# Attention probabilities stored token tile by token tile, and a PV matmul whose moving operand comes in four runs

## The chip, the cores and the metric

The kernel runs on one core of a Trainium2 chip. The metric is the device time of one execution in microseconds (us), as a median over executions. With one core, a run's state is judged by its distance from the fastest run of the same kernel.

The engines are named as in the profile: PE is TensorE (matmuls), PEld its weight loads, DVE is VectorE, ACT is ScalarE, POOL is GpSimd, and SP is the engine that issues most DMAs.

## The reference, cut to what matters

A layer-normed input of 2048 tokens goes through attention with 32 query heads over 8 cached key/value heads, of which the last W = 512 keys count, and through an MLP whose output gates the result.

```python
q = (xn @ wq).reshape(B, Sq, 32, 128).transpose(0, 2, 1, 3)   # B = 1, Sq = 2048
k = jnp.repeat(k_cache[:, :, Sk - 512:, :], 4, axis=1)
v = jnp.repeat(v_cache[:, :, Sk - 512:, :], 4, axis=1)
scores = jnp.einsum("bhqd,bhkd->bhqk", q, k) * (128 ** -0.5)
p = softmax(scores, axis=-1)                                  # the probabilities
o = jnp.einsum("bhqk,bhkd->bhqd", p, v)                       # "PV"
s = o.transpose(0, 2, 1, 3).reshape(B, Sq, 4096) @ wo
out = x + s * g                                               # g: the gate, from the MLP
```

## The kernel before

The tokens are cut into 4 blocks of 512, each block into 4 tiles of 128. One step of the main loop handles one head of one block (128 steps). For each token tile `j`, PE computes the scores of 128 tokens (on the partitions) against 512 keys; ACT takes the exponential and its row sum; DVE divides by the sum. The PV matmuls of this program read the keys on the partitions, so a DMA transpose, the "flip", turns the 16 blocks of 128 x 128 over. Four steps later PE multiplies the flipped probabilities by V, and DVE evicts the result.

```python
def score(s, j):
    h = s % HQ
    if j == 0:
        p_all[s] = work.tile([P, NKC, BLKT, P], BF16, name="p_all", tag="p_all", bufs=4)
        den[s] = work.tile([P, BLKT], FP32, name="den", bufs=3)
    sc = ps.tile([P, W], FP32, name="sc_ps", tag="sc", bufs=4)
    nc.tensor.matmul(sc, qT[s][:, j * P : (j + 1) * P], kT[h // REP], start=True, stop=True)
    nc.scalar.activation(
        p_all[s][:, :, j, :], sc.rearrange("p (kc q) -> p kc q", q=P),
        ACT.Exp, scale=INV_SQRT_DH, accum_out=den[s][:, j : j + 1],
    )

def normalise(s, j0, j1):
    rden = work.tile([P, 2], FP32, name="rden", bufs=4)
    nc.vector.reciprocal(rden, den[s][:, j0 : j1 + 1])
    for j in range(j0, j1 + 1):
        nc.vector.tensor_scalar_mul(
            p_all[s][:, :, j, :], p_all[s][:, :, j, :], rden[:, j - j0 : j - j0 + 1]
        )

def flip(s):
    pT[s] = work.tile([P, NKC, BLK], BF16, name="pT", tag="pT", bufs=4)
    nc.sync.dma_start_transpose(
        pT[s].rearrange("p kc (j q) -> p (kc j) q", q=P), p_all[s][:, :, :, :]
    )

# ... in pv_units, for kc in range(4) (chunks of 128 keys):
    nc.tensor.matmul(
        cur["ps"], v_sb[h // REP][:, kc, :], pT[s][:, kc, :], start=(kc == 0), stop=(kc == NKC - 1)
    )
    # ... after the last one:
    nc.vector.tensor_copy(oT[s // 2][:, s % 2, :], cur["ps"])
```

On each partition, `p_all` holds the 2048 probabilities of four token tiles in the order (key chunk, token tile, key). So the 512 probabilities of one tile lie in four runs of 128, while the flip leaves all 512 tokens of a key chunk in one run for PV.

The softmax here doesn't subtract the row's maximum and nothing guards it: scores larger than these inputs give would overflow.

Of the kernel before, what the change touches and what calls it, by code (L numbers as in the profile page):

```python
# [9 lines left out]
P = 128  # L10
# [3 lines left out]
BF16 = mybir.dt.bfloat16  # L14
# [8 lines left out]
def kernel(  # L23
# [17 lines left out]
    REP = HQ // HKV  # L41
    W = min(4096, max(256, SK // 4))
    NKC = W // P
# [3 lines left out]
    BLKT = 4  # L47
    BLK = BLKT * P
# [15 lines left out]
    work = ctx.enter_context(tc.tile_pool(name="work", bufs=2))  # L64
    ps = ctx.enter_context(tc.tile_pool(name="ps", bufs=1, space=bass.MemoryType.PSUM))
# [14 lines left out]
    v_sb = [res.tile([P, NKC, DH], BF16, name=f"v{g}", tag=f"v{g}") for g in range(HKV)]  # L80
# [119 lines left out]
    p_all = {}  # L200
    pT = {}
# [26 lines left out]
    def score(s, j):  # L228
        h = s % HQ
        if j == 0:  # L230
            p_all[s] = work.tile([P, NKC, BLKT, P], BF16, name="p_all", tag="p_all", bufs=4)
            den[s] = work.tile([P, BLKT], FP32, name="den", bufs=3)
        sc = ps.tile([P, W], FP32, name="sc_ps", tag="sc", bufs=4)
        nc.tensor.matmul(  # L234
            sc, qT[s][:, j * P : (j + 1) * P], kT[h // REP], start=True, stop=True
        )
        nc.scalar.activation(  # L237
            p_all[s][:, :, j, :],
            sc.rearrange("p (kc q) -> p kc q", q=P),
            ACT.Exp,  # L240
            scale=INV_SQRT_DH,
            accum_out=den[s][:, j : j + 1],
        )

    def normalise(s, j0, j1):
        rden = work.tile([P, 2], FP32, name="rden", bufs=4)
        nc.vector.reciprocal(rden, den[s][:, j0 : j1 + 1])  # L247
        for j in range(j0, j1 + 1):
            nc.vector.tensor_scalar_mul(  # L249
                p_all[s][:, :, j, :], p_all[s][:, :, j, :], rden[:, j - j0 : j - j0 + 1]  # L250
            )

    def flip(s):
        pT[s] = work.tile([P, NKC, BLK], BF16, name="pT", tag="pT", bufs=4)
        nc.sync.dma_start_transpose(
            pT[s].rearrange("p kc (j q) -> p (kc j) q", q=P), p_all[s][:, :, :, :]
        )

    s25 = {}
# [1 line left out]
    def row_sums(p):  # L261

        tag = ("kT", "v")[p % 2] + str(p // 2)
        s25[p] = res.tile([P, 2, HALF], BF16, name=f"s25_{p}", tag=tag)
        o = oT[(NBLK - 1) * HQ // 2 + p]
        nc.vector.tensor_tensor(
            out=s25[p].rearrange("p a b -> p (a b)"), in0=o[:, 0, :], in1=o[:, 1, :], op=ALU.add
        )

    def pv_units(s, tag="o"):  # L270
        b, h = divmod(s, HQ)
        cur = {}

        def mm(kc):
            if kc == 0:
                cur["ps"] = ps.tile([P, BLK], FP32, name="o_ps", tag=tag, bufs=1)
            nc.tensor.matmul(  # L277
                cur["ps"], v_sb[h // REP][:, kc, :], pT[s][:, kc, :], start=(kc == 0), stop=(kc == NKC - 1)
            )
            if kc == NKC - 1:  # L280
                if s % 2 == 0:
                    oT[s // 2] = work.tile([P, 2, BLK], BF16, name="oT", tag="oT", bufs=OT_BUFS // 2)
                nc.vector.tensor_copy(oT[s // 2][:, s % 2, :], cur["ps"])  # L283
                if b == NBLK - 1 and s % 2 == 1:
                    row_sums(h // 2)
                del pT[s], p_all[s], qT[s], den[s]

        return [lambda kc=kc: mm(kc) for kc in range(NKC)]
# [326 lines left out]
    with tc.manual_schedule(engines={ENG.PE, ENG.Activation, ENG.DVE, ENG.SP, ENG.Pool}):  # L615
# [161 lines left out]
        for s in range(NSTEP):  # L777
            b, h = divmod(s, HQ)
# [9 lines left out]
            def sc(j):  # L788
                score(s, j)
                if j == 0 and s >= 1:  # L790
                    normalise(s - 1, 2, 3)
                    flip(s - 1)
                if j == 2:
                    normalise(s, 0, 1)
                if j == 3 and s == NSTEP - 1:
                    normalise(s, 2, 3)
                    flip(s)
# [59 lines left out]
```

## Time and profile before

| | before |
|---|---|
| median | 550.09 us (549.88 to 551.0, 3 runs) |
| span of the profiled run | 547.7 us, granted PE clock (the share of its full clock that PE was let have) 1.000 |
| PE, DVE, ACT busy | 99%, 84%, 72% |
| PV matmuls | 512, 379 ns each on the record, 20% of the chain |
| normalising multiplies (DVE) | 512, mean 351 ns |
| exponentials (ACT) | 512, mean 597 ns |

First, lines of the profile page of the kernel before: busy time per engine; the chain of work that ended last; groups of instructions (line, engine, operation, output<-input, shapes, count | busy us, mean ns of one | idle of the engine just before them, and what ended it); and the flip with its median time to landing.

```profile
PE 542.2 (99%) x2676; PEld 261.1 (48%) x2676; DVE 458.4 (84%) x1258; ACT 392.1 (72%) x1125; POOL 20.5 (4%) x41
...
PE 98%; DMA 1%; SPq 0%; DVE 0%; issue 0%
...
L237 ACT ACTIVATE p_all<-sc_ps 128x512 bf16<-128x512 f32 x512 | 305.1, 597 | 104.4 <-PE sc_ps L234 100.4
L249 DVE TENSOR_SCALAR p_all<-p_all,rden 128x512 bf16<-128x512 bf16 x512 | 158.0, 351 | 9.1
L283 DVE CAST oT<-o_ps 128x512 bf16<-128x512 f32 x128 | 88.2, 689 | 35.8 <-PE o_ps L277 35.0
...
L277 PE MATMUL o_ps<-pT,v_100 128*128 128x512 bf16 x64 | 18.4, 379 | 0.0
...
pT<-p_all SPq DMA_TRANSPOSE x128, 4.4
```

A matmul's 379 ns on the record is not what it costs. The records overlap, so the cost is the distance from one start to the next. The records of DVE's multiplies overlap too: 512 of 351 ns would be 180 us, and the group is busy for 158. For PE the table of stages gives the distance (busy us and count per engine, granted clock, DMA share, GB/s):

```profile
core 0: us, PE busy (x) PEld busy (x) DVE busy (x) ACT busy (x) POOL busy (x), PEclk, DMA share, GB/s
...
100.00:240.00 140.00, 139.98 (x650) 63.37 (x649) 111.85 (x298) 101.49 (x290) 2.85 (x5) 1.00 0.86 170
240.00:380.00 140.00, 140.00 (x650) 63.48 (x649) 121.42 (x343) 108.32 (x325) 6.33 (x12) 1.00 0.87 164
```

140 us hold 650 matmuls, one per 215.4 ns, and PE is never idle. The timeline of PE in the kernel before shows the same for one group of PV matmuls (start us, us from the first start to the last end, what, count):

```profile
201.11 1.03 PE L277 MATMUL o_ps<-pT,v_99 128*128 128x512 bf16 x4
201.97 0.38 PE L234 MATMUL sc_ps<-kT_92,qT 128*128 128x512 bf16 x1
```

From 201.11 to 201.97 us is 0.86 us for four matmuls, 215 ns each. This way of reading, the start of the next group less the start of PV's group, divided by four, is used for every experiment below.

Finally, all that PE waited for in the kernel before (engine and line <- who: us, times, longest). Both entries belong to the first microseconds; in the main loop no matmul waits for DVE, ACT or a flip.

```profile
PE warm_ps L642 <- DVE eps L74: 1.2, 1, 1.2
PE h_ps L691 <- DMA w_0_111<-in_B_w_dram: 0.2, 1, 0.2
```

### The profile page before, as it was taken

To read this page: it belongs to the slowest core of one execution; us is meant where nothing else is said; L and a number is where in the kernel's file an instruction comes from. 1 tells how busy PE (TensorE), PEld (TensorE's weight loads), DVE (VectorE), ACT (ScalarE), POOL (GpSimd) and SP (SyncE) were. 2 spreads that over 40 slices of the span, in tenths; PEclk is the share of its full clock that TensorE was granted. 3 is DMA by queue.
4 is the path that set the end of the run, shared out by engine and by line. 5 is a ranking of instruction groups with operands and counts; after the bars stand their busy time and mean duration, and the time that the engine had idled before them with its cause. 6 is when DMAs were issued, how large, how long until landed. Compare 5 with 4: busy or idle time off the path is not lost.

```text
span 547.7 us, 8533 instructions
## 1 busy us (share of the span) xinstructions
PE 542.2 (99%) x2676; PEld 261.1 (48%) x2676; DVE 458.4 (84%) x1258; ACT 392.1 (72%) x1125; POOL 20.5 (4%) x41
## 2 busy tenths in 40 slices
PE   8999999999999999999999999999999999999997
PEld 5644444444444444444444444444444444444586
DVE  6888888887886788898889888988889889988897
ACT  5558757866875677777777777777788888888600
POOL 1000010000000000010001000100010000000010
PEclk9999999999999999999999999999999999999999
DMA  8969769778849799979887988798889778888921
GB/s 260 278 115 186 160 131 165 152 152 159 168 89 193 171 199 226 211 154 193 160 152 145 189 163 143 155 187 161 145 161 183 153 152 156 185 153 154 173 78 40
DMA packets 298909, 89.69 MB, mean 164 GB/s; under 512 B 282352, under 2 KB 297968, under 8 KB 298864
## 3 DMA queue, kind: packets, MB, share of 16 engines
q1 hardware_dynamic: 297056, 85.02, 79.2%
q0 software_dynamic: 1312, 3.67, 2.6%
q10 hardware_dynamic: 496, 0.46, 0.3%
q8 instruction: 21, 0.34, 0.2%
q14 instruction: 24, 0.20, 0.1%
HBM read 17.30 MB, written 2.10 MB: 35 GB/s over the span
## 4 chain that ended last, share of the span: by engine, by line
PE 98%; DMA 1%; SPq 0%; DVE 0%; issue 0%
PE o_ps L277 20%; PE q_ps L212 20%; PE sc_ps L234 20%; PE s_ps L335 15%; PE oB_ps L181 9%; PE h_ps L148 7%; PE m_ps L478 4%; PE h_ps L691 2%; DMA w_0_111<-in_B_w_dram 1%; SPq L622 0%; SPq L618 0%; SPq L623 0%; PE t_ps L658 0%; DVE m_4_6595 L502 0%; DVE x_t L604 0%
## 5 line engine op out<-in xcount | busy, mean ns | idle before, releaser
L237 ACT ACTIVATE p_all<-sc_ps 128x512 bf16<-128x512 f32 x512 | 305.1, 597 | 104.4 <-PE sc_ps L234 100.4
L249 DVE TENSOR_SCALAR p_all<-p_all,rden 128x512 bf16<-128x512 bf16 x512 | 158.0, 351 | 9.1
L283 DVE CAST oT<-o_ps 128x512 bf16<-128x512 f32 x128 | 88.2, 689 | 35.8 <-PE o_ps L277 35.0
L237 ACT ACTIVATION_READ_ACCUMULATOR p_all<-sc_ps 128x1 f32 x512 | 100.4, 196 | 0.0
L224 DVE CAST qT<-q_ps 128x512 bf16<-128x512 f32 x111 | 76.3, 687 | 3.3 <-PE q_ps L212 3.3
L234 PEld LDWEIGHTS <-qT 128*128 128x128 bf16 x512 | 50.1, 98 | 60.5 <-issue 0.2
L335 PEld LDWEIGHTS <-oT 128*128 128x128 bf16 x384 | 37.6, 98 | 45.3
L247 DVE RECIPROCAL rden<-den 128x2 f32<-128x2 f32 x256 | 40.5, 158 | 11.1 <-ACT p_all L237 10.9
L158 ACT ACTIVATE th<-h_ps 128x512 bf16<-128x512 f32 x42 | 25.0, 595 | 4.0 <-PE h_ps L148 3.9
L335 PE MATMUL s_ps<-wo_big_2344,oT 128*128 128x512 bf16 x84 | 26.0, 379 | 0.0
L335 PE MATMUL s_ps<-wo_big_2084,oT 128*128 128x512 bf16 x84 | 26.0, 379 | 0.0
L335 PE MATMUL s_ps<-wo_big_2345,oT 128*128 128x512 bf16 x84 | 26.0, 379 | 0.0
L335 PE MATMUL s_ps<-wo_big_2083,oT 128*128 128x512 bf16 x84 | 26.0, 379 | 0.0
L234 PE MATMUL sc_ps<-kT_91,qT 128*128 128x512 bf16 x64 | 24.3, 379 | 0.0
L234 PE MATMUL sc_ps<-kT_93,qT 128*128 128x512 bf16 x64 | 24.3, 379 | 0.0
L234 PE MATMUL sc_ps<-kT_95,qT 128*128 128x512 bf16 x64 | 24.3, 379 | 0.0
L234 PE MATMUL sc_ps<-kT_94,qT 128*128 128x512 bf16 x64 | 24.3, 379 | 0.0
L234 PE MATMUL sc_ps<-kT_96,qT 128*128 128x512 bf16 x64 | 24.3, 379 | 0.0
L234 PE MATMUL sc_ps<-kT_97,qT 128*128 128x512 bf16 x64 | 24.3, 379 | 0.0
L234 PE MATMUL sc_ps<-kT_92,qT 128*128 128x512 bf16 x64 | 24.3, 379 | 0.0
L234 PE MATMUL sc_ps<-kT_98,qT 128*128 128x512 bf16 x64 | 23.9, 379 | 0.0
L277 PE MATMUL o_ps<-pT,v_100 128*128 128x512 bf16 x64 | 18.4, 379 | 0.0
(316 smaller groups left out, 858.4 us busy)
## 6 DMA issues: line engine op xcount, KB each, us to landing
pT<-p_all SPq DMA_TRANSPOSE x128, 4.4
x_e<-in_A_x_dram POOLq DMA_DIRECT2D x12, 128.0 KB, 3.2
out_dram<-x_e POOLq DMA_DIRECT2D x12, 128.0 KB, 2.3
w_0_113<-in_B_w_dram SPq DMA_DIRECT2D x1, 896.0 KB, 8.9
w_1_114<-in_B_w_dram SPq DMA_DIRECT2D x1, 896.0 KB, 9.8
w_0_111<-in_B_w_dram SPq DMA_DIRECT2D x2, 256.0 KB, 5.1
w_1_112<-in_B_w_dram SPq DMA_DIRECT2D x1, 512.0 KB, 6.9
x_130<-in_A_x_dram SPq DMA_DIRECT2D x1, 512.0 KB, 8.8
```

The lines of the kernel that those rows point to most:

```text
L148: nc.tensor.matmul(h_ps[:, lo : lo + n], w1_sb[f // FH][:, c, (f % FH) * P : (f % FH + 1) * P], xnT[b][:, c, lo : lo + n], start=(c == 0), ...
L158: nc.scalar.activation(th, h_ps, ACT.Tanh, scale=0.5)
L181: nc.tensor.matmul(cur["ps"], hT[b][f // 2][:, f % 2, j * P : (j + 1) * P], w2_sb[f // FH][:, f % FH, :], start=(f == 0), stop=(f == NFC - 1),
L212: nc.tensor.matmul(cur["ps"], wq_sb[h // REP][:, c, (h % REP) * DH : (h % REP + 1) * DH], xnT[b][:, c, :], start=(c == 0), stop=(c == ND - 1),
L224: nc.vector.tensor_copy(qT[s], cur["ps"])
L234: nc.tensor.matmul(sc, qT[s][:, j * P : (j + 1) * P], kT[h // REP], start=True, stop=True)
L237: nc.scalar.activation(p_all[s][:, :, j, :], sc.rearrange("p (kc q) -> p kc q", q=P), ACT.Exp, scale=INV_SQRT_DH, accum_out=den[s][:, j : ...
L247: nc.vector.reciprocal(rden, den[s][:, j0 : j1 + 1])
L249: nc.vector.tensor_scalar_mul(p_all[s][:, :, j, :], p_all[s][:, :, j, :], rden[:, j - j0 : j - j0 + 1])
L277: nc.tensor.matmul(cur["ps"], v_sb[h // REP][:, kc, :], pT[s][:, kc, :], start=(kc == 0), stop=(kc == NKC - 1))
L283: nc.vector.tensor_copy(oT[s // 2][:, s % 2, :], cur["ps"])
L335: nc.tensor.matmul(acc[j], oT[(b * HQ + h) // 2][:, h % 2, j * P : (j + 1) * P], wo_of(h), start=(h == 0), stop=(h == HQ - 1),)
```

## The change

The intent is to let ACT and DVE write and read one run of 512 instead of four runs of 128. The price is that PV reads its moving operand in four runs of 128 (256 bytes), 1 KB apart. The flip covers the same contiguous 2048 columns on both sides; only the meaning of its 16 blocks changes.

```diff
-            p_all[s] = work.tile([P, NKC, BLKT, P], BF16, name="p_all", tag="p_all", bufs=4)
+            p_all[s] = work.tile([P, BLKT, W], BF16, name="p_all", tag="p_all", bufs=4)
@@ exp
-            p_all[s][:, :, j, :],
-            sc.rearrange("p (kc q) -> p kc q", q=P),
+            p_all[s][:, j, :],
+            sc,
@@ multiply
-                p_all[s][:, :, j, :], p_all[s][:, :, j, :], rden[:, j - j0 : j - j0 + 1]
+                p_all[s][:, j, :], p_all[s][:, j, :], rden[:, j - j0 : j - j0 + 1]
@@ flip
-        pT[s] = work.tile([P, NKC, BLK], BF16, name="pT", tag="pT", bufs=4)
+        pT[s] = work.tile([P, BLKT, NKC, P], BF16, name="pT", tag="pT", bufs=4)
-            pT[s].rearrange("p kc (j q) -> p (kc j) q", q=P), p_all[s][:, :, :, :]
+            pT[s].rearrange("p j kc q -> p (j kc) q"), p_all[s].rearrange("p j w -> p (j w)")
@@ PV
-                cur["ps"], v_sb[h // REP][:, kc, :], pT[s][:, kc, :], ...
+                cur["ps"], v_sb[h // REP][:, kc, :], pT[s][:, :, kc, :], ...
```

The two built programs, compared instruction by instruction, differ in 1536 places and in access patterns only: the output of 512 exponentials, both sides of 512 multiplies, and the moving operand of 512 PV matmuls. The score in PSUM is read as one run in both, and the flips are identical. Order and semaphores are the same.

More of the change, by code (lines that the diff above doesn't have):

```diff
@@ L277, in mm @@
             nc.tensor.matmul(
-                cur["ps"], v_sb[h // REP][:, kc, :], pT[s][:, kc, :], start=(kc == 0), stop=(kc == NKC - 1)
+                cur["ps"], v_sb[h // REP][:, kc, :], pT[s][:, :, kc, :], start=(kc == 0), stop=(kc == NKC - 1)
             )
```

## The prediction

> **What bounds the kernel now.** TensorE. The page's busy table gives PE 542.2 us of the 547.7 us span (99%), and the chain of waits is PE for 98%. In the table of stages PE is busy 139.98 of 140.00 us between 100 and 240 us, with 650 matmuls at a granted clock of 1.00: one per 215.4 ns.[...] PE's own waits sum to 1.4 us. DVE is busy 84%, ACT 72%, DMA queue 1 79%, but in the view of who waited for whom no matmul of the main loop waits for them.
>
> **What the change does.** The two built programs, compared by instruction, have the same 8,031 instructions in the same order with the same semaphores. Only access patterns differ, in three groups of 512.
>
> 1. Exp on ACT (mean 597 ns) writes one run of 512 instead of four of 128. Tanh of the same size, which already writes one run, takes 595 ns. Change: 0 to -2 ns each.
> 2. The normalising multiply on DVE (mean 351 ns, 158 us in all) reads and writes one run. Estimates from the trace: bf16 tensor_tensor takes 285, 422, 553 and 687 ns for 256, 512, 768 and 1024 elements: about 153 ns fixed[...]; runs of 256 lie on that line, so breaks are free there.[...] centering x, one run with two pointer scalars, takes 407. [...]I expect 340 to 352 ns. Were breaks what makes 351 out of 287, DVE would save at most 33 us, all off the critical path.
> 3. PV's moving operand becomes four runs of 128 bf16 (256 B), 1 KB apart. These 512 matmuls are 20.2% of the chain (512 x 215.4 ns = 110 us): the only term on the critical path. The trace has no matmul with such an operand.[...] I expect 0 to 2 ns per matmul, 0 to 1 us in all.
>
> The flip moves the same 16 blocks between the same addresses; its 4.4 us to landing should stay.
>
> **Predicted time:** 550.2 us, range 548.5 to 553.5 us. Faster by over 2%: 1%. Within 2%: 94%. Slower by over 2%: 5%.
>
> **What would show each step right or wrong.**
> - PV durations stay at 379 ns and their share of the chain at 20.2%; 650 matmuls fill 140 us. If PV grows, step 3 is wrong: 10 ns per PV matmul would be 5 us, 21 ns would pass 2%.
> - The multiply's mean at 340 to 352 ns; near 290 would mean that breaks did cost DVE, and its busy share would fall to about 78% with the span unchanged.
> - Exp at 595 to 597 ns; flip 4.4 us; no new PE wait.
>
> **What would make it wrong.** A fixed cost on PE for every break in the moving operand: at three breaks per matmul, 7 ns each is 2%. Or reads by PE at 1 KB steps[...], seen as spread in the PV durations (now 377 to 380 ns). Or a faster DVE that starts flips in another rhythm; nothing on PE waits for flips today, with four heads of lag, so that should not surface.

Passages of this text that no trace of this case showed are cut, with the cut marked, and terms of step 2's sum go with them. The sum came to about 347 ns: 153 fixed, 134 for 512 elements at half the 0.52 ns per element of the tensor_tensor rows, and about 60 for the pointer scalar; without the last it is the 287 that the text still names. The 0.52 is (687 - 285) / 768; the half of it was assumption, and so was the 60, the rest of 351 less 287. The total, 550.2 us, is within 0.2 us of the medians of the kernel before (550.09 and 550.04 us): steps 1 and 2 were put off the critical path, and step 3 added 0 to 1 us.

## The result

The changed kernel takes 549.90 us (median of 6 runs, 549.69 to 550.27); the kernel before, run beside it, 550.04 us (6 runs, 549.84 to 551.0). The ratio is 0.9997, with a 95% interval of 0.9984 to 1.0009: the same time. Ratios here and below are the mean time of one kernel's fast runs over the mean of the other's in the same rounds, so they are not quite the ratios of the quoted medians.

The page of the changed kernel, the same lines as above:

```profile
PE 542.3 (99%) x2676; PEld 261.5 (48%) x2676; DVE 458.1 (84%) x1258; ACT 391.9 (72%) x1125; POOL 20.5 (4%) x41
...
PE 99%; DVE 0%; ACT 0%; issue 0%
...
L237 ACT ACTIVATE p_all<-sc_ps 128x512 bf16<-128x512 f32 x512 | 305.1, 597 | 104.5 <-PE sc_ps L234 100.5
L249 DVE TENSOR_SCALAR p_all<-p_all,rden 128x512 bf16<-128x512 bf16 x512 | 157.9, 351 | 9.1
L283 DVE CAST oT<-o_ps 128x512 bf16<-128x512 f32 x128 | 88.2, 689 | 35.9 <-PE o_ps L277 35.2
...
L277 PE MATMUL o_ps<-pT,v_105 128*128 128x512 bf16 x64 | 18.4, 379 | 0.0
...
pT<-p_all SPq DMA_TRANSPOSE x128, 4.4
```

The table of stages, PE's timeline around one PV group, and PE's waits, all of the changed kernel:

```profile
100.00:240.00 140.00, 139.98 (x650) 63.33 (x648) 111.82 (x299) 101.23 (x290) 3.08 (x5) 1.00 0.88 170
240.00:380.00 140.00, 140.00 (x650) 63.47 (x649) 121.39 (x343) 108.52 (x325) 6.09 (x12) 1.00 0.87 165
```

```profile
200.87 1.03 PE L277 MATMUL o_ps<-pT,v_99 128*128 128x512 bf16 x4
201.74 0.38 PE L234 MATMUL sc_ps<-kT_92,qT 128*128 128x512 bf16 x1
```

```profile
PE warm_ps L642 <- DVE eps L74: 1.2, 1, 1.2
```

No instruction that the change touches became longer or shorter, to the nanosecond of its mean: 597, 351 and 379 ns before and after. Four PV matmuls still take 0.87 us to the next start; summed over all 512 PV matmuls of the trace, the distances to the next start are 110.6 us before and after. The 0.3 us between the two profiled spans (547.7 and 547.4 us) are within the spread of single runs.

The trace therefore shows no two opposed effects. The open questions are why a break between runs is free, how far that holds, and whether the time would have moved had DVE gained.

### The profile page after: what moved, and what is told of

Read it like the earlier page. It is cut to its first block, busy times and chain, and to the rows that moved or that the text cites. A ratio compares the mean times of both kernels' runs of the same rounds, so it can differ in the third digit from the quotient of the medians.

```text
span 547.4 us, 8533 instructions
## 1 busy us (share of the span) xinstructions
PE 542.3 (99%) x2676; PEld 261.5 (48%) x2676; DVE 458.1 (84%) x1258; ACT 391.9 (72%) x1125; POOL 20.5 (4%) x41
## 4 chain that ended last, share of the span: by engine, by line
PE 99%; DVE 0%; ACT 0%; issue 0%
PE sc_ps L234 20%; PE q_ps L212 20%; PE o_ps L277 20%; PE s_ps L335 15%; PE oB_ps L181 9%; PE h_ps L148 7%; PE m_ps L478 4%; PE h_ps L691 2%; PE warm_ps L642 1%; PE t_ps L649 0%; PE t_ps L658 0%; DVE m_4_6595 L502 0%; DVE x_t L604 0%; ACT xnT_107 L653 0%; DVE warm L68 0%
## 5 line engine op out<-in xcount | busy, mean ns | idle before, releaser
L249 DVE TENSOR_SCALAR p_all<-p_all,rden 128x512 bf16<-128x512 bf16 x512 | 157.9, 351 | 9.1
```

The source lines that it names most:

```text
L249: nc.vector.tensor_scalar_mul(p_all[s][:, j, :], p_all[s][:, j, :], rden[:, j - j0 : j - j0 + 1])
```

## The experiments

Theory: breaks between runs of 256 bytes cost nothing on any of the three engines; and PE's stream of matmuls alone sets the time, so DVE's and ACT's times do not matter. Rivals: a small loss on PE is paid back by a small gain elsewhere; or breaks do cost, too little to be seen at three per instruction; or DVE is part of what sets the time.

Twelve kernels ran, all against the kernel before. The three that compute wrong values (half_pv, half_prob, mul_imm) still came back as correct: the scores of this input are small, the softmax is nearly flat, and presumably the tolerance does not see whose key block was used (this was not tested). Correctness therefore proves nothing for those three. In the other nine it does not prove much more about which key is which, but their patterns are permutations of tokens or elementwise, and a wrong token order would be a wrong output row.

### The two halves of the change (half_pv, half_prob)

half_pv is the kernel before with only PV's new reading:

```diff
-   cur["ps"], v_sb[h // REP][:, kc, :], pT[s][:, kc, :], ...
+   cur["ps"], v_sb[h // REP][:, kc, :], pT[s].rearrange("p kc (j q) -> p kc j q", q=P)[:, :, kc, :], ...
```

> Only PV's part of the change: the kernel before, but each PV matmul reads four runs of 128 columns 1 KB apart, as in the changed kernel; it therefore reads blocks that belong to other keys, a wrong result on purpose. Theory (a break in the moving operand costs TensorE nothing, and every other part of the change costs nothing either): ratio to before 1.000 within 0.2%, PV matmuls 379 ns, PV 20.2% of the chain. Rival (PV got dearer and ACT or DVE paid it back, so that the sum is zero): this half alone is slower, by 0.5% or more, with PV matmuls above 379 ns or waits on PE.

Measured: 550.05 us against 550.18 us, ratio 0.9994 (0.9982 to 1.0007). PV is 20% of the chain, and its matmuls take 379 ns:

```profile
L277 PE MATMUL o_ps<-pT,v 128*128 128x512 bf16 x512 | 145.1, 379 | 0.3
```

half_prob is the changed kernel with PV reading one run of 512 again:

```diff
-   cur["ps"], v_sb[h // REP][:, kc, :], pT[s][:, :, kc, :], ...
+   cur["ps"], v_sb[h // REP][:, kc, :], pT[s].rearrange("p j kc q -> p (j kc q)")[:, kc * BLK : (kc + 1) * BLK], ...
```

> Only the probabilities' part of the change: exp and the multiply in one run of 512, flip as in the changed kernel, but PV reads one run of 512, hence the wrong blocks, a wrong result on purpose. Theory: ratio 1.000 within 0.2%, multiply 351 ns, exp 597 ns. Rival (the sum of the change is zero because this half gains): faster by 0.5% or more.

Measured: 549.95 us against 550.18 us, ratio 0.9991 (0.9977 to 1.0005); multiply 351 ns, exp 597 ns. Neither half moves the time, so the zero of the whole is not a sum of a loss and a gain. That rival falls. (The traces of half_pv, half_prob, pv_runs8 and pv_step8 lack 45 to 48 of the 2676 matmul records, while all 2676 weight loads are there, so matmuls per stage are not counted from these four.)

### How far a break is free on PE (pv_runs8, pv_step8, pv_runs2, pv_step2, pv_step4)

These are the kernel before with PV's 512 columns read in another order. The eviction writes them back to their places, so the result is right. The edit of pv_runs8; the others differ only in the pattern:

```diff
-   cur["ps"], v_sb[h // REP][:, kc, :], pT[s][:, kc, :], ...
+   cur["ps"], v_sb[h // REP][:, kc, :], pT[s][:, kc, :].rearrange("p (c r e) -> p r c e", r=8, e=8), ...
-   nc.vector.tensor_copy(oT[s // 2][:, s % 2, :], cur["ps"])
+   nc.vector.tensor_copy(
+       oT[s // 2][:, s % 2, :].rearrange("p (c r e) -> p r c e", r=8, e=8),
+       cur["ps"].rearrange("p (r c e) -> p r c e", r=8, e=8),
+   )
# pv_runs2: r=16, e=2.  pv_step8, pv_step4, pv_step2: "p (c r) -> p r c" with r=8, 4, 2
```

The first two:

(Cut from this group's expectations is a rule about reads within 16 bytes that no trace had shown. The slowing expected of pv_step8 and the 379 ns expected of pv_runs2 came from it, and so did a third value for pv_step4, 379 ns, which is cut with it. pv_step8's rival, also without its reason now, was that the 215 ns of a matmul's 512 columns, 0.42 ns per column, stay whatever the step.)

> The kernel before with PV's moving operand read as 64 runs of 8 columns (16 bytes each), 128 bytes apart, so 63 breaks instead of the 3 of the change; the eviction writes the columns back to their places, so the result is right. Theory (breaks are free): PV matmuls 379 ns, ratio 1.000 within 0.5%. Rival (each break costs TensorE a little, too little to see at 3): 21 times the breaks; already 1 ns a break would be 63 ns per matmul, 512 x 63 = 32 us, ratio about 1.06. The eviction on DVE should stay at 689 ns if a strided write costs nothing.

> The kernel before with PV's moving operand read one column at a time at steps of 16 bytes (8 rows of 64 columns)[...]; the eviction puts the columns back, the result is right. Theory[...]: this one must be slower, PV matmuls clearly over 379 ns, 512 x 200 ns = 100 us or more if the rate halves. Rival[...]: 379 ns and ratio 1.000 within 0.5%.

pv_runs8: 549.75 us against 550.18 us, ratio 0.9991 (0.9977 to 1.0004); PV 379 ns, eviction 689 ns. Sixty-three breaks per matmul are as free as three; PE's timeline of pv_runs8:

```profile
200.72 1.03 PE L277 MATMUL o_ps<-pT,v 128*128 128x512 bf16 x4
201.58 0.38 PE L234 MATMUL sc_ps<-kT,qT 128*128 128x512 bf16 x1
```

pv_step8: 976.58 us, ratio 1.7736 (1.7692 to 1.778). So the layout of the moving operand can matter, and a great deal. Lines of PE's timeline in pv_step8, early and later, and its groups of PV matmuls and evictions:

```profile
62.31 1.06 PE L277 MATMUL o_ps<-pT,v 128*128 128x512 bf16 x1
63.19 0.40 PE L148 MATMUL h_ps<-xnT,w 128*128 128x512 bf16 x1
...
298.23 3.76 PE L277 MATMUL o_ps<-pT,v 128*128 128x512 bf16 x4
301.81 0.40 PE L234 MATMUL sc_ps<-kT,qT 128*128 128x512 bf16 x1
```

```profile
L277 PE MATMUL o_ps<-pT,v 128*128 128x512 bf16 x512 | 494.4, 1070 | 1.7 <-DVE oT L283 1.4
L283 DVE CAST oT<-o_ps 128x512 bf16<-128x512 f32 x128 | 312.4, 2441 | 246.3 <-PE o_ps L277 246.2
```

Four PV matmuls take 3.58 us, 895 ns each instead of 215. Over 512 of them that is 348 us of the 423 us by which the profiled span grew (970.3 against 547.7 us). The granted clock falls to 0.89 to 0.92 in the stages after 240 us, but that is not what makes PV slow: at 62 us, in a stage with a granted clock of 1.00, a single PV matmul already takes 880 ns to the next start. The rest of the growth, some 75 us, lies in the other matmuls, which do lengthen in those stages (s_ps to a mean of 482 ns, from 379). The eviction, now writing single elements 16 bytes apart, takes 2441 ns, but PE waits for it for only 1.4 us in all. The ratio of this run is therefore not PV's cost alone.

The next three runs were to tell what is being paid for.

> The kernel before with PV's moving operand in runs of 2 columns (4 bytes), each run 64 bytes from the last, 255 breaks per matmul; the eviction puts the columns back, the result is right. Single columns 16 bytes apart cost 1070 ns per PV matmul where 8 columns per 16 bytes cost 379. Theory[...]: PV matmuls 379 ns on the record, ratio about 1.00, unless the eviction holds TensorE. Rival (what counts is the number of lines touched, 256 here against 512 single columns): about half of the extra 690 ns, so 700 to 750 ns per PV matmul and a ratio near 1.3. The eviction, at 689 ns with runs of 8 and 2441 with single columns, should lie between.

> The kernel before with PV's moving operand read at every second column (4 bytes apart, two rows of 256), result right. Line theory, fitted to the two slow runs (425 ns per PV matmul start to start with 2 columns per 16 bytes, about 900 with 1, i.e. about 1.67 ns for each visit to a new 16-byte line against 0.42 ns per column, whichever is longer): here 4 columns come from each line, so 379 ns on the record and ratio 1.000 within 0.5%. Rival (every step that is not to the next column costs): 511 such steps per matmul, as many as in the run with 16-byte steps, so near 1070 ns and a ratio near 1.7.

> The kernel before with PV's moving operand read at every fourth column (8 bytes apart, four rows of 128), result right. Line theory with 16-byte lines: 2 columns per line, as in runs of 2, so 600 ns on the record, 425 ns start to start, ratio 1.20. The same theory with 8-byte lines: 1070 ns, ratio near 1.7.[...]

pv_runs2: 659.37 us against 549.86 us, ratio 1.1985 (1.1964 to 1.2005). pv_step2: 555.42 us against 550.06 us, ratio 1.0103 (1.0088 to 1.0118). pv_step4: 670.72 us against 550.06 us, ratio 1.2197 (1.2177 to 1.2217). PE's timelines, in that order:

```profile
301.53 1.88 PE L277 MATMUL o_ps<-pT,v 128*128 128x512 bf16 x4
303.23 0.40 PE L234 MATMUL sc_ps<-kT,qT 128*128 128x512 bf16 x1
```

```profile
300.30 1.07 PE L277 MATMUL o_ps<-pT,v 128*128 128x512 bf16 x4
301.20 0.38 PE L234 MATMUL sc_ps<-kT,qT 128*128 128x512 bf16 x1
```

```profile
301.50 1.97 PE L277 MATMUL o_ps<-pT,v 128*128 128x512 bf16 x4
303.29 0.40 PE L234 MATMUL sc_ps<-kT,qT 128*128 128x512 bf16 x1
```

The five runs and the change side by side. A "line" here and in the expectations is 16 bytes in a row of the operand on one partition, 8 bf16 columns: a unit for counting, fitted to these times; no trace shows how the operand is fetched. "Line visits" counts how often the stream of 512 columns enters another line; the last two columns compare (start-to-start less 215.4 ns) x 512 with the growth of the span over 547.7 us.

| pattern | columns per 16-byte line | line visits | non-unit steps | start to start | x 512 | span grew by |
|---|---|---|---|---|---|---|
| before, one run of 512 | 8 | 64 | 0 | 215 ns | 0 | 0 |
| the change, 4 runs of 128 | 8 | 64 | 3 | 217 ns | 1 us | -0.3 us |
| runs of 8 | 8 | 64 | 63 | 215 ns | 0 | -0.4 us |
| every 2nd column | 4 | 128 | 511 | 225 ns | 5 us | 5.2 us |
| runs of 2 | 2 | 256 | 255 | 425 ns | 107 us | 109.4 us |
| every 4th column | 2 | 256 | 511 | 447 ns | 119 us | 120.6 us |
| every 8th column | 1 | 512 | 511 | 895 ns | 348 us | 422.6 us |

(The 217 ns of the change come from 0.87 us read to two decimals; its stage table has the same 650 matmuls in 140 us as before, and the sum over all PV matmuls is the same.)

In these runs time follows the line visits, not the number of breaks: with 511 non-unit steps the cost goes from 10 ns to 680 ns as the columns per line fall from 4 to 1, and 255 and 511 steps cost nearly the same when both have 2 columns per line. As an estimate, about 1.7 ns per line visit (425 / 256, 895 / 512) against 0.42 ns per column (215 / 512), whichever is longer, fits the table to within about 5%. What makes the 22 ns between the two patterns with 256 visits is open. pv_step4 and pv_runs2 also settle the length to count by: with 8-byte lines pv_step4 would have cost as much as pv_step8 (447 against 895 ns), and with 32-byte lines pv_runs2 would have (425 against 895). Of the expectations, both of pv_runs2 missed: its PV matmuls took 600 ns on the record, between the 379 and the 700 to 750 that were expected. I had expected exactly nothing of pv_step2; its 10 ns per matmul, 1.03% of the time, is a small miss: 128 visits at 1.7 ns are 218 ns by the fit, just above the 215 of the columns. The line theory was right for pv_step4 (425 ns expected, 447 measured).

Breaks between runs that fill their lines cost nothing here: 215 ns with 63 of them, as with none. In the terms of the fit the columns are then the longer of the two: 64 visits would take about 110 ns, an estimate, half of the 215 ns that the columns take anyway. That is the margin in which the change sits.

### DVE: is the multiply at its fast rate, and does its time matter? (mul_imm, mul_step2, mul_runs2, mul_runs8)

All four are the changed kernel with another multiply. Its factor is a "pointer scalar", one value per partition read from memory; mul_imm puts a constant into the instruction instead. "The tensor_tensor rate" is that of the rows in the prediction, about 0.52 ns per element (687 less 285 ns over 768 elements); "the double rate" is twice that, 0.26 ns. These expectations: the assumption of step 2 that the multiply runs at the double rate, and that it falls to the tensor_tensor rate at a step of 2 (267 ns in mul_step2's sum, where step 2 has 134) but not in runs of 2. No trace had shown either. The rivals were that its 351 ns are already the tensor_tensor rate, with a smaller fixed part.

```diff
-   p_all[s][:, j, :], p_all[s][:, j, :], rden[:, j - j0 : j - j0 + 1]
# mul_imm
+   p_all[s][:, j, :], p_all[s][:, j, :], 1.0 / W
# mul_runs2, mul_runs8, mul_step2: both tensors as
+   p_all[s][:, j, :].rearrange("p (c r e) -> p r c e", r=16, e=2)     # runs2; r=8, e=8 for runs8
+   p_all[s][:, j, :].rearrange("p (c r) -> p r c", r=2)               # step2
```

> The changed kernel with the multiply's pointer scalar replaced by the constant 1/512 in the instruction; the reciprocals still run. Wrong on purpose (the true sums differ a little from 512). Theory[...]: 285 to 295 ns, DVE's busy time about 30 us lower, 78% of the span, and the time unchanged (ratio 1.000 within 0.2%) because DVE is not on the chain. Rival[...]: stays above 330 ns. Rival on the chain (DVE holds TensorE somewhere): faster by 0.5% or more.

> The changed kernel with the multiply's innermost step set to 2 elements (2 rows of 256), result right. Theory[...]: 153 + 267 + 60 = about 480 ns. Rival ([...]layout has no say): 351 ns. DVE then has about 66 us more, 95% busy; the ratio shows whether TensorE's slack covers that: by the theory that DVE is off the chain with one or two heads of lag to spare, under 1.02.

> The changed kernel with the multiply reading and writing runs of 2 elements (4 bytes), 64 bytes apart, 255 breaks instead of none; the result is right. Theory (a break is free for DVE too[...]): 351 ns. Rival (DVE, like TensorE and like the eviction in the run with single columns, pays for each new 16-byte line): 256 lines instead of 64 each way, 600 ns or more; then DVE has over 500 us of work, 256 multiplies' worth of 0.25 us more, and TensorE begins to wait: ratio 1.05 or more.

> The changed kernel with the multiply in 64 runs of 8 elements (16 bytes, 128 bytes apart), result right. With 256 runs of 2 the multiply took 443 ns instead of 351. Line theory (a run that fills its 16-byte line costs nothing more): 351 ns, within 5. Rival (each break costs alike): 92 ns over 255 breaks is 0.36 ns a break, so 351 + 63 x 0.36 = 374 ns; the change's 3 breaks would then be 1 ns, below what the trace shows. Time: ratio 1.000 within 0.5% either way.

Measured, against 549.86 us (the first three) and 550.11 us (mul_runs8):

| run | median | ratio (95%) | DVE busy | multiply |
|---|---|---|---|---|
| mul_imm | 549.62 us | 0.9994 (0.998 to 1.0008) | 75% | 280 ns |
| mul_runs8 | 550.27 us | 0.9998 (0.9974 to 1.0021) | 84% | 351 ns |
| mul_runs2 | 552.92 us | 1.0049 (1.0034 to 1.0065) | 90% | 443 ns |
| mul_step2 | 558.24 us | 1.0147 (1.0131 to 1.0162) | 92% | 513 ns |

The multiplies of mul_imm, mul_runs8 and mul_step2, in that order, and mul_imm's stage from 240 to 380 us:

```profile
L249 DVE TENSOR_SCALAR p_all<-p_all 128x512 bf16<-128x512 bf16 x512 | 121.6, 280 | 0.0
L249 DVE TENSOR_SCALAR p_all<-p_all,rden 128x512 bf16<-128x512 bf16 x512 | 157.9, 351 | 9.1
L249 DVE TENSOR_SCALAR p_all<-p_all,rden 128x512 bf16<-128x512 bf16 x512 | 234.1, 513 | 9.1
```

```profile
240.00:380.00 140.00, 140.00 (x650) 63.46 (x649) 105.08 (x343) 108.68 (x326) 6.00 (x11) 1.00 0.89 165
```

Without the pointer scalar the multiply takes 280 ns, 7 below the estimate of 287 and 5 below the range on record. The scalar costs 71 ns, not about 60 (80 for the first multiply of each pair, 61 for the second). The time of a tensor_tensor of 512 elements (422 ns) is far above that of the multiply with a constant; with the same 153 ns fixed, 280 ns leave 0.25 ns per element, an estimate at about the double rate. That the multiply with a pointer scalar also runs at the double rate is not shown by mul_imm alone, for the scalar itself could have set a slower one: within a pair, one multiply starts 268 ns after the other, which is just 512 elements at the tensor_tensor rate. mul_step2, below, speaks against that: there the distance is 405 ns, longer by 137, where a fall from the double to the tensor_tensor rate takes 134 by the 0.52 ns. So by these two runs together the multiply ran at about the double rate, an estimate. It took 351 ns with four runs as with one, and the new layout had nothing to give to DVE.

DVE's busy time fell by 50.3 us against the changed kernel (458.1 to 407.8), more than the 36.3 us of the group (157.9 to 121.6), and more than the 30 or so on record. The rest is overlap: a multiply that no longer needs the reciprocal's result starts 83 ns before the reciprocal's record ends, in all 256 pairs, where none overlapped in the changed kernel (21 us; overlaps elsewhere shrink by about 7). The edit thus removed a dependency as well as the scalar. In the stage shown 16 us of DVE work are gone (121.39 to 105.08) and PE does its 650 matmuls in 140 us as before: had the change made DVE faster, the time would not have moved.

mul_step2 gives the other direction. Its chain of waits by engine, and the same stage:

```profile
PE 69%; DVE 25%; issue 4%; DMA 1%; ACT 1%; ACTq 0%
```

```profile
240.00:380.00 140.00, 137.20 (x634) 61.91 (x633) 134.97 (x337) 105.73 (x318) 7.00 (x12) 1.00 0.86 161
```

The multiply went from 351 to 513 ns when its innermost step became 2, 33 more than my estimate of 480. The time rose by 1.5%, within what I had allowed. In this stage DVE is at 96% (134.97 of 140 us), PE gets 634 matmuls done instead of 650, and a quarter of the chain is now DVE. With the multiply at 443 ns (mul_runs2) the same stage holds 642 matmuls, and PE's waits show it waiting for DVE's evictions a few times, 1.9 us in all. So DVE's 16% of idle time before the change was mostly slack, but not all of it: half a per cent of time was lost at 90% busy. "Off the chain" was right for a DVE made faster; neither of the two slower ones was free.

For mul_runs2 both expectations missed. Breaks were to be free (351 ns) or to cost over 250 ns; they cost 92. mul_runs8 shows that the break itself is not what is paid: 63 breaks, 351 ns, where a fixed price per break would have given 374. What DVE pays for in runs of 2 was not shown, and no experiment has runs between 4 and 16 bytes.

DVE's evictions out of PSUM went differently, and I leave open why: they took 689 ns when they wrote one run or runs of 8, 691 in runs of 2, 729 at every second, 1303 at every fourth and 2441 at every eighth element.

### ACT (exp_runs2)

```diff
-            p_all[s][:, j, :],
-            sc,
+            p_all[s][:, j, :].rearrange("p (c r e) -> p r c e", r=16, e=2),
+            sc.rearrange("p (c r e) -> p r c e", r=16, e=2),
```

> The changed kernel with exp reading and writing runs of 2 elements (8 bytes of scores in PSUM, 4 bytes of probabilities, 64 bytes apart), result right. Theory ([...]the change of the exp's layout could not matter): 597 ns within 5 ns, ratio 1.000 within 0.5%. Rival (ACT pays for new lines as TensorE does): over 700 ns, and the time rises once ACT's 72% passes TensorE's share.

Measured: 550.19 us against 550.06 us, ratio 1.0004 (0.999 to 1.0019). The exponential:

```profile
L237 ACT ACTIVATE p_all<-sc_ps 128x512 bf16<-128x512 f32 x512 | 310.2, 607 | 104.0 <-PE sc_ps L234 100.1
```

Even 255 breaks cost ACT 10 ns, a little outside the 5 ns and far below the rival's 100. The three breaks that the change removed had no cost to remove: 597 ns before and after.

## Why the prediction was right

- **Time.** Predicted 550.2 us (548.5 to 553.5), "within 2%" at 94%; measured 549.90 us. Right.
- **PE bounds the kernel, and nothing else does.** Right for the change, with less room on DVE than the 84% suggest: 92 ns more per multiply cost half a per cent (mul_runs2). A multiply shortened by 71 ns moved nothing; PV matmuls lengthened by 10, 210 and 232 ns moved the span by 5.2, 109.4 and 120.6 us, about what 512 of them add up to.
- **Step 1, exp: 0 to -2 ns.** Right: 597 ns both times; 255 breaks cost 10 ns.
- **Step 2, multiply: 340 to 352 ns.** Right: 351. The reasoning, the double rate plus a pointer scalar, was an assumption; mul_imm (280 ns without the scalar) and mul_step2 (513 ns) together agree with it. Its parts were 7 ns too high and 11 ns too low, and nearly cancelled, which was luck. The alternative it allowed for, that breaks turn 287 into 351, is excluded by the unchanged 351 and by mul_runs8.
- **Step 3, PV: 0 to 2 ns per matmul.** Right: 379 ns on the record and the same number of matmuls per stage. What the runs show is that breaks between runs that fill their 16 bytes cost nothing (215 ns), while two columns per line about doubled the distance (425 and 447 ns), and four came within 5% of the 215 (225 ns).
- **Flip: 4.4 us to landing, nothing on PE waits for it.** Right, by the page and by PE's waits.
- **What would make it wrong.** A price per break of the moving operand was named as the first danger. None was seen for full lines (215 ns with 63 breaks). What was seen, by the fit about 1.7 ns per line visited, cost 109 us with runs of 2, and nothing with the runs of 8 and of 128. Of the other two dangers, trouble with reads at 1 KB steps was to show as spread in PV's durations (377 to 380 ns before, 377 to 379 after: none was seen), and a DVE made faster moved nothing in mul_imm.

## What to carry to other kernels

Ask two things of a layout change before anything else: which of the touched instructions lie on the chain, and whether its present layout slows any of them; here one of three was on the chain, and none was slowed by its breaks, so there was nothing to win. A moving operand in runs that fill 16-byte lines cost nothing here, with 4 runs as with 64. With four bf16 columns per line PE lost 5% per matmul (225 ns against 215), with two half its speed (425 and 447 ns), with one three quarters (895 ns), and what the matmuls on the chain lost down to two columns per line was paid in full (5.2, 109.4 and 120.6 us). Making an engine faster that the chain of waits does not name gained nothing here (DVE from 84% to 75% busy, ratio 0.9994), but such an engine can hold the chain well before its average reaches 100%: here a DVE at 90% already cost half a per cent.
